# Softmax scaling on GpSimd instead of VectorE, and one f tile in halves, in a dynamic convolution feeding a two-matmul block

## The chip, the cores and the metric

The kernel runs on one core of a Trainium2 chip. The metric is the device time of one execution in microseconds (us). Ten executions of the kernel before had a median of 772.5 us (771.71 to 773.02). Engines are called TensorE (PE in the profile, PEld for its weight loads), VectorE (DVE), ScalarE (ACT), GpSimd (POOL) and SyncE (SP, whose queue issues most DMAs).

## The reference

`x` is (8, 4096, 192) and `weight_gen` is (8, 4096, 8 heads, 7 taps), both float32. Each token has its own softmaxed 7-tap filter per head; the filter runs causally over the sequence, and its output feeds two matmuls with `h - tanh(h)` between them:

```
w = exp(weight_gen - max);  w = w / (sum(w, -1) + 1e-9)
out[b,s,h,:] = sum_k  w[b,s,h,k] * x_pad[b, s+k, h, :]     # 6 zeros in front, 24 channels a head
h = out.reshape(32768, 192) @ w_in          # w_in (192, 2048)
y = (h - tanh(h)) @ w_out                   # w_out (2048, 192), float32 out
```

## The kernel before, in words

Tokens are worked on in 32 *superblocks* of 1024 (`TOK`): partition p holds 8 consecutive tokens (`J`), with a halo of 6 rows in front of them (`HALO`). Four superblocks make one sequence, so every fourth one (`s == 0`) begins with zeros instead of a halo. For each superblock n:

- `load_wg(n)` and `load_x(n)` bring the filter logits and x (with halo) to SBUF through SP's DMA queue. x tiles have two buffers.
- `softmax_exp(n)` takes the exponential on ScalarE (L135). `softmax_norm` (L150) does the rest on VectorE: a sum over taps (L145), a reciprocal (L154), and the *scaling*, exp times reciprocal (L172). The reciprocal is written into the unused end of a PSUM bank: that of the transposes for n >= 4, one of the output banks for 0, 1 and 3. Superblock 2 has a variant, `softmax_norm_gpsimd`, with the reciprocal in SBUF (L166) and the scaling on GpSimd.
- `products(n)` multiplies x, shifted by tap, with the scaled weights: seven products (L195), written in bf16 to `even`, `odd` and `last`. They run on GpSimd, save four of superblock 0 and two of superblock 1, which VectorE does (`on_vector`) with a second copy of the scaled weights in PSUM. From superblock 3 on, a DMA issued by GpSimd (L208) adds `odd` to `even`, the *pair sum*.
- `conv(n)` sums the products and transposes them in one go: matmuls against an identity (L240) accumulate in PSUM, in two parts (channel chunks 0 and 1, then 2), and ScalarE copies them to `convT` (L251).
- `gemm1(n, f)` makes one *f tile*, 128 of the 2048 hidden features for all 1024 tokens: six matmuls (L265) into a PSUM tile `ph`, tanh on ScalarE (L275), subtraction on VectorE into `gt` (L277).
- `gemm2` multiplies 128 tokens of the superblock before with `w_out` (L297), and ScalarE copies the result out (L315); the last superblock has `gemm2_last` (L331).

The order is written out by hand (`manual_schedule`); each engine runs its instructions in program order. The main loop takes superblock n in eight steps p. A step is f tiles 2p and 2p+1, then one block of gemm2 for n-1. At p = 0 the products of n+2 are issued, and from n = 2 on their first one carries an extra dependency, the *pace*: it waits for the subtraction of f tile 1. At p = 5 comes the exponential of n+3, at p = 6 (n >= 2) the transposes of n+1 and then the softmax of n+3.

`ph` and the two PSUM tiles of the transposes (`pc`) come in turn from one pool, `psum_h`, of three buffers. Eighteen tiles a superblock are drawn from it, so in steady state the first part of the transposes takes the buffer of f tile 11, the second that of 12, f tile 14 that of 13, 15 that of the first part, tile 0 of the next superblock that of the second part, and tile 1 that of 14. Each waits until the readers of its predecessor are done.

Weights: `load_w_in` brings `w_in` in two pieces of columns (split at `FA`) to partitions 0 to 63 through GpSimd's queue, and `copy_w_in` copies each piece to partitions 64 to 127, the first from ScalarE's queue, the second from SP's.

Of the kernel before, what the change touches and what calls it, by code (L numbers as in the profile page):

```python
# [16 lines left out]
def kernel(  # L17
# [81 lines left out]
    def load_x(n):  # L99
        b, s = divmod(n, NSB)  # L100
        s0 = s * TOK

        x_t = xpool.tile([P, HALO + J, D], FP32, name="x_t")

        def rows(p0, p1):
            win = x[b, s0 + p0 * J - HALO : s0 + p0 * J - HALO + 1]
            nc.sync.dma_start(
                out=x_t[p0:p1, :, :],
                in_=bass.AP(
                    tensor=win.tensor,  # L110
                    offset=win.offset,
                    ap=[[J * D, p1 - p0], [D, HALO + J], [1, D]],
                ),
            )

        if s == 0:
            nc.sync.dma_start(  # L117
                out=x_t[0:1, 0:HALO, :],
                in_=zero[:].rearrange("o (h d) -> o h d", h=1).to_broadcast([1, HALO, D]),
            )  # L120
            nc.sync.dma_start(
                out=x_t[0:1, HALO : HALO + J, :],
                in_=x[b, 0:J].rearrange("(p j) d -> p j d", p=1),
            )

            rows(1, 16)
            rows(16, P)
        else:
            rows(0, P)
        x_of[n] = x_t  # L130
# [8 lines left out]
        )  # L139
        e_of[n] = e_t  # L140

    def softmax_sum(n):
        e_t = e_of.pop(n)
        zsum = wgpool.tile([P, J * H], FP32, name="zsum")
        nc.vector.reduce_sum(  # L145
            out=zsum[:], in_=e_t[:].rearrange("p j h k -> p (j h) k"), axis=AX.X
        )
        return e_t, zsum

    def softmax_norm(n, bank, in_psum=False):  # L150

        e_t, zsum = softmax_sum(n)
        zr = bank[:, 512 - J * H : 512]
        nc.vector.reciprocal(zr, zsum[:])  # L154
        wsm_v = None
        if in_psum:
            wsm_v = obank[n % 2][:, 0 : J * H * K].rearrange("p (j h k) -> p j h k", j=J, h=H)
            scale(nc.vector, wsm_v, e_t, zr)
        wsm = wgpool.tile([P, J, H, K], FP32, name="wsm")
        last_wsm[0] = scale(nc.vector, wsm[:], e_t, zr)  # L160
        wsm_of[n] = (wsm, wsm_v)

    def softmax_norm_gpsimd(n):
        e_t, zsum = softmax_sum(n)
        zr = wgpool.tile([P, J * H], FP32, name="zr")
        nc.vector.reciprocal(zr[:], zsum[:])  # L166
        wsm = wgpool.tile([P, J, H, K], FP32, name="wsm")
        scale(nc.gpsimd, wsm[:], e_t, zr[:])
        wsm_of[n] = (wsm, None)

    def scale(eng, wsm, e_t, zr):
        return eng.tensor_mul(  # L172
# [2 lines left out]
            zr.rearrange("p (n o) -> p n o", o=1).to_broadcast([P, J * H, K]),  # L175
        )

    def products(n, on_vector=(), sums=None, hooks={}, behind=None):
        x_t = x_of.pop(n)
        wsm, wsm_v = wsm_of.pop(n)  # L180
        in_pairs = n not in PLAIN

        even = ppool.tile([P, NPAIR, NC, J, H, GC], BF16, name="even")
        odd = ppool.tile([P, NPAIR, NC, J, H, GC], BF16, name="odd")
        last = ppool.tile([P, NC, J, H, GC], BF16, name="last")
        dst = {}
        for i in range(NPAIR):
            dst[2 * i] = even[:, i]
            dst[2 * i + 1] = odd[:, i]
        dst[K - 1] = last[:]  # L190
        if -1 in hooks:
            hooks[-1]()
        for k in range(K):
            eng, w = (nc.vector, wsm_v) if k in on_vector else (nc.gpsimd, wsm[:])
            mul = eng.tensor_mul(  # L195
                dst[k].rearrange("p c j h g -> p j h c g"),
                x_t[:, k : k + J, :].rearrange("p j (h c g) -> p j h c g", h=H, c=NC),
                w[:, :, :, k : k + 1]
                .rearrange("p j h (k o) -> p j h k o", o=1)
                .to_broadcast([P, J, H, NC, GC]),  # L200
            )
            if k == 0 and behind is not None:


                order(mul, behind, "pace")
            if k == K - 2 and in_pairs:

                nc.gpsimd.dma_start(  # L208
                    out=even[:].rearrange("p i c j h g -> p (i c j h g)")[:, 0:ACC],
                    in_=odd[:].rearrange("p i c j h g -> p (i c j h g)")[:, 0:ACC],  # L210
                    accum_op=mybir.AluOpType.add,
                    max_dma_last_dim=4096,
                )
            if k in hooks:
                hooks[k]()
        if in_pairs:
            groups = [even[:, i] for i in range(NPAIR)] + [last[:]]
            prods_of[n] = [
                groups + ([odd[:, NPAIR - 1]] if c == NC - 1 else []) for c in range(NC)
            ]  # L220
        else:
            prods_of[n] = [[dst[k] for k in (sums or range(K))]] * NC

    def conv(n, *parts):

        prods = prods_of[n]
        if n not in conv_of:
            conv_of[n] = cpool.tile([P, NC, HT], BF16, name="convT")
        convT = conv_of[n]
        pcs = [psum_h.tile([P, 2, HT], FP32, name="pc", tag="ph") for _ in parts]  # L230

        for gi in range(max(len(g) for g in prods)):
            for chunks, pc in zip(parts, pcs):
                some = [c for c in chunks if gi < len(prods[c])]
                last = gi == max(len(prods[c]) for c in chunks) - 1
                for c in some:
                    for j in range(JH):
                        col = ((c - chunks[0]) * JH + j) * R
                        for r in range(2):
                            nc.tensor.matmul(  # L240
                                pc[:, r, col : col + R],
                                lhsT=prods[c][gi][
                                    r * R : (r + 1) * R, c, 2 * j : 2 * j + 2
                                ].rearrange("p j h g -> p (j h g)"),
                                rhs=ident[r * R : (r + 1) * R, r * R : (r + 1) * R],
                                start=(gi == 0 and c == chunks[0] and j == 0),
                                stop=(last and c == some[-1] and j == JH - 1),
                            )
        for chunks, pc in zip(parts, pcs):
            c0, nch = chunks[0], len(chunks)  # L250
            nc.scalar.activation(  # L251
                out=convT[:, c0 : c0 + nch, :].rearrange("p c (j r t) -> p r (c j) t", r=2, t=R),
                in_=pc[:, :, 0 : nch * JH * R].rearrange("p r (cj t) -> p r cj t", t=R),
                func=ACT.Copy,
            )
        if parts[-1][-1] == NC - 1:
            prods_of.pop(n)
        return pcs[-1][:, 0]

    def gemm1(n, f):  # L260
        convT = conv_of[n]
        ph = psum_h.tile([P, 2, HT], FP32, name="ph", tag="ph")
        for c in range(NC):
# [8 lines left out]
        th = tpool.tile([P, TOK], FP32, name="th")  # L272
        ph_f = ph[:].rearrange("p r t -> p (r t)")
        g1_act[0] = last_act.get(0)
        last_act[0] = nc.scalar.activation(out=th[:], in_=ph_f, func=ACT.Tanh)  # L275
        gt = gpool.tile([P, TOK], BF16, name=f"gt{f}", tag=f"gt{f}")
        last_sub[0] = nc.vector.tensor_sub(gt[:], ph_f, th[:])  # L277
        g_of.setdefault(n, []).append(gt)

    LAST = (NTOT - 1) * J  # L280
# [76 lines left out]
    def load_w_out():  # L357
        nc.gpsimd.dma_start(out=w_out[:], in_=moe_w_out.rearrange("(c p) e -> p c e", c=NFT))

    FA = 8 * P  # L360

    def load_w_in(f0, f1):

        for c in range(NC):
            src = moe_w_in[c * GC : c * GC + 1, f0:f1]
            dma = nc.gpsimd.dma_start(
                out=w_in[0:R, c, f0:f1],
                in_=bass.AP(
                    tensor=src.tensor, offset=src.offset, ap=[[G * F, H], [F, GC], [1, f1 - f0]]
                ),  # L370
            )
            if f0 == 0:

                order(dma, last_wsm[0], "order of the loads")
# [4 lines left out]
    def rest_of_w_in():  # L379
# [2 lines left out]
    load_wg(0)  # L382
    load_x(0)
    softmax_exp(0)
    softmax_norm(0, obank[0], in_psum=True)
    load_wg(1)
    load_x(1)
    load_w_in(0, FA)
    products(
        0,  # L390
        on_vector=(3, 4, 5, 6),
        sums=(3, 0, 4, 5, 1, 6, 2),
        hooks={2: rest_of_w_in},
    )
    softmax_exp(1)
    softmax_norm(1, obank[1], in_psum=True)
    load_wg(2)
    copy_w_in(0, FA, nc.scalar)
    copy_w_in(FA, F, nc.sync)
# [3 lines left out]
    for n in range(NTOT):  # L403
# [1 line left out]
            load_wg(n + 3)  # L405
            load_x(n + 3)
        for p in range(J):
            gemm1(n, 2 * p)
            gemm1(n, 2 * p + 1)
            if n == 0 and p == 1:  # L410
                softmax_exp(2)
# [6 lines left out]
            if n + 1 < NTOT:  # L418
                if p == (6 if n > 0 else 7):
                    conv(n + 1, (0, 1))  # L420
                if p == (6 if n > 1 else 7):
                    bank = conv(n + 1, (2,))
            if n == 0 and p == 2:
                softmax_norm_gpsimd(2)
                products(2)
            if p == (7 if n == 1 else 6) and n + 3 < NTOT:

                softmax_norm(n + 3, bank if n > 0 else obank[0])
    gemm2(LAST)
    for j in range(J):  # L430
        gemm2_last(j)
# [30 lines left out]
```

The softmax here doesn't subtract the row's maximum and nothing guards it: scores larger than these inputs give would overflow.

## Time and profile before

| | |
|---|---|
| median of ten runs | 772.5 us |
| profiled execution | 772.88 us, its span 770.8 us |
| TensorE busy | 741.4 us, 96% of the span |
| VectorE busy | 668.9 us, 87% |
| ScalarE busy | 640.4 us, 83% |
| GpSimd busy | 668.1 us, 87% |
| subtraction (L277) | 512 times 1219 ns |
| tanh (L275) | 512 times 1022 ns |
| scaling on VectorE to SBUF (L172) | 31 times, 620 to 622 ns |
| scaling on GpSimd (L172) | once, 968 ns |
| product on GpSimd (L195) | 218 times, start to start 2.86 us |
| pair sum (L208), issue to landing | 29 times, 8.0 / 8.9 / 10.5 us (least, median, most) |

The span runs from the first to the last instruction of the profiled execution. Busy time counts an instruction from start to end; where consecutive instructions of one engine overlap, the distance between their starts says more. An idle time in brackets is what the engine stood still just before an instruction, with the engine that ended it.

### The profile page before, as it was taken

The page shows a single profiled execution, that of the slowest core. Times are in us where ns is not written, and L with a number is a line of the kernel's source. Part 1 is how long each engine was busy: PE and PEld are TensorE (multiplying, and loading weights), DVE is VectorE, ACT ScalarE, POOL GpSimd, SP SyncE. Part 2 cuts the span into 40 slices and gives each one's busy share as a digit, 9 for nine tenths or more (in the row PEclk, how much of TensorE's full clock was granted, in tenths as well). Part 3 has the DMA queues.
Part 4 walks back from the last instruction along what each step waited for, and adds up shares of the span by engine and source line. Part 5 has one row for each costly group of instructions (what it writes and reads, how often), then busy time and mean ns, then how long its engine had stood idle before and what let it go on. Part 6 is the DMA issues. An engine that isn't in the chain of part 4 may idle for free.

```text
span 770.8 us, 32309 instructions
## 1 busy us (share of the span) xinstructions
PE 741.4 (96%) x14784; PEld 578.8 (75%) x14784; DVE 668.9 (87%) x624; ACT 640.4 (83%) x865; POOL 668.1 (87%) x261
## 2 busy tenths in 40 slices
PE   2789999999999999999999999999999999999997
PEld 2367777777787777778777777777777777778777
DVE  5988889988989898899888998989898988988883
ACT  1777888888888888888888888888888888888882
POOL 5999999999999999999999999999999999999000
PEclk9999999999999999999999999999999999999999
DMA  7913677665557765556765555775555776542312
GB/s 208 192 71 92 177 182 181 157 139 127 152 154 181 182 140 131 136 149 172 181 170 117 131 153 158 181 180 126 135 142 149 178 181 153 133 117 64 82 43 83
DMA packets 25847, 111.37 MB, mean 144 GB/s; under 512 B 4800, under 2 KB 9456, under 8 KB 21624
## 3 DMA queue, kind: packets, MB, share of 16 engines
q1 hardware_dynamic: 14688, 76.95, 30.2%
q0 software_dynamic: 10816, 31.99, 25.7%
q8 instruction: 115, 1.88, 1.0%
q10 hardware_dynamic: 208, 0.39, 0.2%
q14 instruction: 20, 0.16, 0.1%
HBM read 54.49 MB, written 25.17 MB: 103 GB/s over the span
## 4 chain that ended last, share of the span: by engine, by line
PE 93%; DVE 2%; DMA 1%; POOL 1%; issue 1%; ACT 1%; SPq 0%; POOLq 0%; DVEq 0%
PE ph L265 43%; PE obank L297 43%; PE pc L240 6%; DVE gt L277 2%; PE po L331 1%; DMA x_t<-in_x_dram 1%; POOL even L195 1%; ACT convT L251 0%; ACT th L275 0%; POOL odd L195 0%; DVE wsm L172 0%; DVE zsum L145 0%; SPq L117 0%; DVE pc L154 0%; DVE obank L154 0%
## 5 line engine op out<-in xcount | busy, mean ns | idle before, releaser
L277 DVE TENSOR_TENSOR gt<-ph,th 128x1024 bf16<-128x1024 f32 x512 | 602.8, 1219 | 64.0 <-ACT th L275 63.7
L275 ACT ACTIVATE th<-ph 128x1024 f32<-128x1024 f32 x512 | 497.2, 1022 | 65.1 <-PE ph L265 64.7
L265 PE MATMUL ph<-convT,w_in 64*128 64x512 bf16 x3072 | 386.6, 378 | 7.3 <-DVE gt L277 5.0
L297 PEld LDWEIGHTS <-gt 64*128 64x128 bf16 x7936 | 344.4, 94 | 52.3 <-ACT th L275 0.8
L297 PE MATMUL obank<-w_out,gt 64*128 64x192 bf16 x7936 | 374.0, 243 | 1.4 <-issue 0.6
L195 POOL TENSOR_TENSOR even<-x_t,wsm 128x1536 bf16<-128x1536 f32 x94 | 276.8, 2945 | 30.6 <-DVE gt L277 28.6
L195 POOL TENSOR_TENSOR odd<-x_t,wsm 128x1536 bf16<-128x1536 f32 x93 | 273.8, 2944 | 0.0
L265 PEld LDWEIGHTS <-w_in 64*128 64x128 bf16 x3072 | 176.5, 94 | 117.4 <-issue 21.3
L195 POOL TENSOR_TENSOR last<-x_t,wsm 128x1536 bf16<-128x1536 f32 x31 | 103.4, 3334 | 0.0
L315 ACT ACTIVATE out_sb<-obank 128x192 f32<-128x192 f32 x248 | 81.9, 330 | 13.9 <-PE obank L297 8.6
L251 ACT ACTIVATE convT<-pc 128x1024 bf16<-128x1024 f32 x64 | 48.6, 808 | 30.7 <-PE pc L240 30.7
L240 PE MATMUL pc<-ident,even 64*128 64x64 bf16 x2304 | 47.4, 191 | 2.9 <-DVE gt L277 1.5
L240 PEld LDWEIGHTS <-even 64*128 64x128 bf16 x2304 | 42.5, 96 | 3.8 <-issue 1.9
L208 POOL DMA_DIRECT2D even<-odd x29 | 34.9, 1205 | 9.0 <-POOL odd L195 9.0
L154 DVE RECIPROCAL pc<-zsum 128x64 f32<-128x64 f32 x28 | 15.7, 561 | 14.7 <-ACT convT L251 14.6
L240 PE MATMUL pc<-ident,odd 64*128 64x64 bf16 x448 | 15.2, 198 | 13.0 <-DVE odd L195 13.0
L135 ACT ACTIVATE e_t<-wg_t 128x448 f32<-128x448 f32 x32 | 18.5, 577 | 8.3 <-DMA wg_t<-in_weight_gen_dram 8.3
L240 PE MATMUL pc<-ident,last 64*128 64x64 bf16 x768 | 23.1, 191 | 0.8 <-issue 0.7
L145 DVE TENSOR_REDUCE zsum<-e_t 128x64 f32<-128x448 f32 x32 | 19.5, 610 | 2.8 <-ACT e_t L135 2.8
L240 PEld LDWEIGHTS <-odd 64*128 64x128 bf16 x448 | 11.2, 100 | 13.2 <-DVE odd L195 13.1
L172 DVE TENSOR_TENSOR wsm<-e_t,pc 128x448 f32<-128x448 f32 x28 | 17.4, 622 | 2.9
L240 PEld LDWEIGHTS <-last 64*128 64x128 bf16 x768 | 17.0, 96 | 1.1 <-issue 0.8
(22 smaller groups left out, 51.4 us busy)
## 6 DMA issues: line engine op xcount, KB each, us to landing
x_t<-in_x_dram SPq DMA_DIRECT2D x24, 1344.0 KB
even<-odd POOLq DMA_DIRECT2D x29, 1024.0 KB, 8.9
out_dram<-out_sb SPq DMA_DIRECT2D x31, 768.0 KB
x_t<-in_x_dram SPq DMA_DIRECT2D x8, 1176.0 KB
wg_t<-in_weight_gen_dram SPq DMA_DIRECT2D x32, 224.0 KB
x_t<-in_x_dram SPq DMA_DIRECT2D x8, 157.5 KB
w_in<-in_moe_w_in_dram POOLq DMA_DIRECT2D x6, 128.0 KB, 7.0
w_out<-in_moe_w_out_dram POOLq DMA_DIRECT2D x1, 768.0 KB, 9.7
```

The source lines that it names most:

```text
L135: nc.scalar.activation(out=e_t[:].rearrange("p j h k -> p (j h k)"), in_=wg_t[:].rearrange("p j h k -> p (j h k)"), func=ACT.Exp,)
L145: nc.vector.reduce_sum(out=zsum[:], in_=e_t[:].rearrange("p j h k -> p (j h) k"), axis=AX.X)
L172: return eng.tensor_mul(wsm.rearrange("p j h k -> p (j h) k"), e_t[:].rearrange("p j h k -> p (j h) k"), zr.rearrange("p (n o) -> p n o", ...
L195: mul = eng.tensor_mul(dst[k].rearrange("p c j h g -> p j h c g"), x_t[:, k : k + J, :].rearrange("p j (h c g) -> p j h c g", h=H, c=NC), ...
L208: nc.gpsimd.dma_start(out=even[:].rearrange("p i c j h g -> p (i c j h g)")[:, 0:ACC], in_=odd[:].rearrange("p i c j h g -> p (i c j h g)" ...
L240: nc.tensor.matmul(pc[:, r, col : col + R], lhsT=prods[c][gi][r * R : (r + 1) * R, c, 2 * j : 2 * j + 2].rearrange("p j h g -> p (j h g)") ...
L251: nc.scalar.activation(out=convT[:, c0 : c0 + nch, :].rearrange("p c (j r t) -> p r (c j) t", r=2, t=R), in_=pc[:, :, 0 : nch * JH * R].re ...
L265: nc.tensor.matmul(ph[:, r, :], lhsT=w_in[r * R : (r + 1) * R, c, f * P : (f + 1) * P], rhs=convT[r * R : (r + 1) * R, c, :], start=(c == ...
L275: last_act[0] = nc.scalar.activation(out=th[:], in_=ph_f, func=ACT.Tanh)
L277: last_sub[0] = nc.vector.tensor_sub(gt[:], ph_f, th[:])
L297: mm = nc.tensor.matmul(po[:, 0:D], lhsT=g_of[n][f][r * R : (r + 1) * R, col : col + P], rhs=w_out[r * R : (r + 1) * R, f, :], start=(r == ...
L315: last_act[0] = nc.scalar.activation(out=out_sb[:, j, :], in_=po[:, 0:D], func=ACT.Copy)
```

## The change

- *Scaling.* The normalisation of superblocks 0 and 1 stays as it was, on VectorE. For all others `softmax_norm(n)` now ends with the reciprocal, in an SBUF tile; the scaling is issued on GpSimd as the first instruction of `products(n)`, and the pace is put on it instead of on the first product. The softmax of n+3 stands at p = 6 in every superblock (n = 1 had it at p = 7).
- *Halves.* f tile 12 of superblocks 1 to 30, the first of the two f tiles of the step that ends with the transposes, goes through tanh and subtraction in two halves of 512 tokens.
- *Beginning.* x of superblock 0 is loaded first without halo for all partitions, then the halo in two pieces, then the zeros of partition 0. Its products are issued in the order 6, 0, 3, 1, 4, 5, 2 (VectorE: 6, 3, 4, 5; GpSimd: 0, 1, 2), and the transposes sum them in the order 6, 3, 0, 4, 5, 1, 2. The first piece of `w_in` has seven f tiles instead of eight, the second nine.

```diff
+        def rows(p0, p1, r0=0, r1=HALO + J):
+            win = x[b, s0 + p0 * J - HALO + r0 : s0 + p0 * J - HALO + r0 + 1]
...
+        if n == 0:
+            rows(0, P, HALO, HALO + J)
+            rows(16, P, 0, HALO)
+            rows(1, 16, 0, HALO)
+            no_halo()
+        elif s == 0:
+            no_halo()
+            rows(0, 1, HALO, HALO + J)
             rows(1, 16)
             rows(16, P)
...
-    def softmax_norm(n, bank, in_psum=False):
+    def softmax_norm(n, bank=None):
         e_t = e_of.pop(n)
         zsum = wgpool.tile([P, J * H], FP32, name="zsum")
         nc.vector.reduce_sum(...)
+        wsm = wgpool.tile([P, J, H, K], FP32, name="wsm")
+        if bank is None:
+            zr = wgpool.tile([P, J * H], FP32, name="zr")
+            nc.vector.reciprocal(zr[:], zsum[:])
+            wsm_of[n] = (wsm, None, e_t, zr)
+            return
...
-    def products(n, on_vector=(), sums=None, hooks={}, behind=None):
+    def products(n, on_vector=(), order_of=None, sums=None, hooks={}, behind=None):
         x_t = x_of.pop(n)
-        wsm, wsm_v = wsm_of.pop(n)
+        wsm, wsm_v, e_t, zr = wsm_of.pop(n)
+        if e_t is not None:
+            first = scale(nc.gpsimd, wsm[:], e_t, zr[:])
+            if behind is not None:
+                order(first, behind, "pace")
...
-        for k in range(K):
+        for k in order_of or range(K):
...
-            if k == 0 and behind is not None:
-                order(mul, behind, "pace")
...
-    def gemm1(n, f):
+    def gemm1(n, f, parts=1):
...
-        last_act[0] = nc.scalar.activation(out=th[:], in_=ph_f, func=ACT.Tanh)
-        last_sub[0] = nc.vector.tensor_sub(gt[:], ph_f, th[:])
+        for q in range(parts):
+            t0, t1 = q * TOK // parts, (q + 1) * TOK // parts
+            last_act[0] = nc.scalar.activation(
+                out=th[:, t0:t1], in_=ph_f[:, t0:t1], func=ACT.Tanh
+            )
+            last_sub[0] = nc.vector.tensor_sub(gt[:, t0:t1], ph_f[:, t0:t1], th[:, t0:t1])
...
-    FA = 8 * P
+    FA = 7 * P
...
-        on_vector=(3, 4, 5, 6),
-        sums=(3, 0, 4, 5, 1, 6, 2),
+        on_vector=(6, 3, 4, 5),
+        order_of=(6, 0, 3, 1, 4, 5, 2),
+        sums=(6, 3, 0, 4, 5, 1, 2),
...
-            gemm1(n, 2 * p)
+            gemm1(n, 2 * p, 2 if p == 6 and 0 < n < NTOT - 1 else 1)
...
-            if p == (7 if n == 1 else 6) and n + 3 < NTOT:
-                softmax_norm(n + 3, bank if n > 0 else obank[0])
+            if p == 6 and n + 3 < NTOT:
+                softmax_norm(n + 3)
```

## The prediction

> **What bounds the kernel now.** I read the page first (busy time, then the chain that ended last), and then the timeline of one superblock from the middle. From the page:
>
> ```profile
> PE 741.4 (96%) x14784; PEld 578.8 (75%) x14784; DVE 668.9 (87%) x624; ACT 640.4 (83%) x865; POOL 668.1 (87%) x261
> PE 93%; DVE 2%; DMA 1%; POOL 1%; issue 1%; ACT 1%; SPq 0%; POOLq 0%; DVEq 0%
> ```
>
> TensorE carries 93% of the chain. A change of VectorE or GpSimd work can therefore pay only where TensorE waits for them. The timeline around one set of transposes (L240) shows where that is; columns: start us, duration us, engine, line, instruction, and in brackets the idle time before it.
>
> ```profile
> 361.18 1.48 PE L265 MATMUL ph<-convT,w_in 64*128 64x512 bf16 x12
> ...
> 363.11 2.36 DVE L277 TENSOR_TENSOR gt<-ph,th 128x1024 bf16<-128x1024 f32 x2 [0.26 <-ACT th L275]
> ...
> 363.80 0.88 PE L240 MATMUL pc<-ident,even 64*128 64x64 bf16 x48
> ...
> 365.51 1.47 PE L265 MATMUL ph<-convT,w_in 64*128 64x512 bf16 x12
> 366.37 1.94 ACT L275 ACTIVATE th<-ph 128x1024 f32<-128x1024 f32 x2
> 366.49 0.56 DVE L154 RECIPROCAL pc<-zsum 128x64 f32<-128x64 f32 x1 [0.51 <-ACT convT L251]
> ...
> 367.16 0.62 DVE L172 TENSOR_TENSOR wsm<-e_t,pc 128x448 f32<-128x448 f32 x1
> 367.69 4.71 DVE L277 TENSOR_TENSOR gt<-ph,th 128x1024 bf16<-128x1024 f32 x4
> ...
> 368.13 1.67 PE L265 MATMUL ph<-convT,w_in 64*128 64x512 bf16 x12
> ...
> 370.93 1.48 PE L265 MATMUL ph<-convT,w_in 64*128 64x512 bf16 x12
> ```
>
> A regular step (two f tiles and one output block) is 2.61 us, as from 358.57 to 361.18. Eight steps (20.92) and the transposes (1.52 in the chain) make 22.44. But the same row returns every 22.82 us (365.51, 388.33). The missing 0.38 has two halves.
> (a) Transposes start at 363.80, so the next f tile (14) could start at 365.32; it starts at 365.51. It takes the PSUM buffer of tile 13, whose subtraction ends at 363.11 + 2.36 = 365.47: a wait of 0.19.
> (b) 368.13 to 370.93 is 2.80, 0.19 too long. Tile 1 of the new superblock takes the buffer of tile 14, whose subtraction starts at 367.69, late, behind the reciprocal and the scaling. As a check: superblock 29 has transposes but no softmax behind them, and its period (707.95 to 730.58) is 22.63, exactly (b) less.
>
> GpSimd, third:
>
> ```profile
> 36.32 0.97 POOL L172 TENSOR_TENSOR wsm<-e_t,zr 128x448 f32<-128x448 f32 x1
> 37.37 2.90 POOL L195 TENSOR_TENSOR even<-x_t,wsm 128x1536 bf16<-128x1536 f32 x1
> ...
> 78.59 3.35 POOL L195 TENSOR_TENSOR even<-x_t,wsm 128x1536 bf16<-128x1536 f32 x1
> ...
> 100.16 3.36 POOL L195 TENSOR_TENSOR even<-x_t,wsm 128x1536 bf16<-128x1536 f32 x1
> ...
> 349.66 2.90 POOL L195 TENSOR_TENSOR even<-x_t,wsm 128x1536 bf16<-128x1536 f32 x1 [1.19 <-DVE gt L277]
> ```
>
> Unpaced, GpSimd's round is 100.16 - 78.59 = 21.57; later it waits about 1.19 per round for the pace. The one scaling that it does today takes it 37.37 - 36.32 = 1.05 from start to start.
>
> [...] the scaling at 36.32 ran beside back-to-back subtractions, so 1.05 holds for the loop. [...]
>
> **The change part by part.**
>
> *Scaling off VectorE (29 scalings, those of 3 to 31, issued in superblocks 0 to 28; that of 2 was on GpSimd already).* It removes 0.62 us and the reciprocal's 0.51 wait for the copy of the transposes, since the reciprocal now goes to SBUF (0.55, row L166). Sum and reciprocal run 365.38 to about 366.55; VectorE is then free, and tile 14's subtraction starts when its tanh ends (366.37 + 1.02, about 367.43) instead of at 367.69. That alone would lift (b), but with (a) lifted too tile 14 starts earlier, while ScalarE still copies the transposes until 366.46 and can't start its tanh before 366.37. I leave 0.08 of the 0.19 standing: gain 0.11 in 27 superblocks, 3.0 us.
>
> *Tile 12 in halves (n = 1 to 30).* Tanh of 512 columns costs about 0.59 (row convT 128x512), so two take about 0.06 more ScalarE time than one of 1.02[...]. The first half can start at about 362.8 (when tile 11's is done) instead of 363.11, so tile 13's subtraction is no longer queued behind tile 12's but starts when its own tanh ends, 0.15 earlier. Gain 0.15 of (a)'s 0.19 in 29 superblocks (2 to 30; superblock 1 splits its transposes otherwise, taken as nothing): 4.35 us.
>
> *Scaling on GpSimd, pace ahead of it.* 21.57 + 1.05 = 22.62 per round, against TensorE's new 22.56. The 1.19 of pace wait covers it, and more: products never catch up with the pace after superblock 4, so that wait is gone and GpSimd runs without a break. Does the conv then wait for products? Products(4) would start near 78.9 (78.59 + 1.05 - 0.7 from the beginning), products(31) at 78.9 + 27 x 22.62 = 689.6; the pair sum is issued 1.05 + 17.5 later and lands 8.9 (median row) to 10.5 after that: 717.1 to 718.7. The last transposes, at 728.86 now, come at about 720.5. So the cover is 2 to 3.5 us at the end. Behind products on SP stand the x load, an output store and a weight_gen load; each moves later by GpSimd's lag behind the pace, at most 6 us by these starts, and each has over 10 us until its reader (the x load about 22.6 less its landing). Without cover the kernel would end at GpSimd's speed: 717.9 + 42 (what follows the last transposes now) = 760 span.
>
> *Beginning.* x of superblock 0 comes without halo first, then the halo; the two tiny transfers no longer stand ahead. VectorE can start k = 6 near 7 to 8 us; GpSimd starts k = 0, which needs the halo, near 9.8 instead of 10.52 (bounds: 9.3, if all of the 1.2 us that SP spends on the tiny ones, 1.19 to 2.43, is won; 10.7, if the shorter rows cost as much as that), and its three products still end last on the way to the transposes. Tile 0 of the first matmul at 20.92 also waited for the copy of w_in (1.05, landing 20.9), which is 7/8 as big now. I take 0.6 for both. The second part of w_in, 9/8 as big, is now needed for tile 7 (at 30.0 now): its copy was issued at 26.02, the first one took 3.7 us, so it lands at about 29.5: cost 0.3 (0 to 1.0). VectorE sets the pace in superblock 0 (12 waits of L265 for L277, 5.0 us, nearly all before 41 us); it loses one scaling: 0.6. Superblock 2's first step loses 0.2 of (b).
>
> *Sum.* 3.0 + 4.35 + 0.6 + 0.6 + 0.2 - 0.3 = 8.4. Span 770.8 - 8.4 = 762.4; its execution 772.88 - 8.4 = 764.5. Against the median of ten, 772.5, that is 764.1.
>
> **Rivals.**
> 1. *Both halves of the wait vanish and GpSimd becomes the bound.* Period 22.44 would give 28 x 0.38 + 1.1 = 11.7 off, but products for 31 land at 717.9: end at 760 span, 762 measured; with the early landing 760.5. For it: my residues 0.08 and 0.04 are small differences of large numbers. Against: ScalarE's copies stay where they are. 15%.
> 2. *The halves do nothing.* If the second half waits as long as the whole did, only the scaling pays: (b) goes fully, 27 x 0.19 + 1.1 = 6.2: 766.3, or 769 if the beginning also loses 1.6 us, to w_in's second copy above all, where I have it gain 1.1. For it: the idle that it uses is 0.26 only[...]. 17%.
> 3. *Slower: the scaling is dearer in the loop.* GpSimd then sets the period. Its end is 728.9 + 29 x s - 0.7 for a start-to-start price s; it equals 770.8 at s = 1.47. At s = 1.7 it is 777.5 span, 779 measured. For it: only one sample of s exists. Against: it was taken beside busy VectorE. 9%.
> 4. *Nothing moves,* since a new wait of the same size replaces each: 772 +- 1.5. The 22.63 of superblock 29 speaks against it. 4%.
>
> **How the numbers follow.** Main case 55% (762.5 to 766, its range from w_in's 0 to 1.0, the beginning's bounds and residues of 0 to 0.1), rivals 15, 17, 9 and 4. Rivals 1 and 2 and the main case are faster: 87%; rival 4 is same, rival 3 slower. 0.2% is 1.5 us, about what this kernel's runs can tell. The range goes from rival 1's lower end, 760.3, to 769, rival 2's far end.
>
> **What would show it.** GpSimd's pace waits go from 28.6 us to nearly nothing; a GpSimd scaling row x30 of about 0.97; GpSimd rounds of 22.6; TensorE period 22.5 to 22.6; reciprocals without a wait for convT; tile 14's tile pair starting under 1.58 us after the transposes. Wrong: transposes waiting for GpSimd or for the pair sum in the last third; a scaling above 1.2; a tile-7 wait over 1 us near 30 us.

## The result, and the profile after

The changed kernel takes 788.47 us (median; 788.12 to 788.58) against 772.73 of the kernel before: a ratio of 1.0203, with a 95% interval of 1.0194 to 1.0212. It is 15.7 us slower; 764.1 was predicted, 760.3 to 769.0. The profiled span grew from 770.8 to 785.8.

First the page of the changed kernel: busy time with the number of instructions, then the chain that ended last.

```profile
PE 740.1 (94%) x14784; PEld 581.9 (74%) x14784; DVE 657.5 (84%) x625; ACT 641.0 (82%) x895; POOL 696.2 (89%) x290
PE 69%; DVE 18%; ACT 8%; issue 3%; POOL 1%; DMA 0%
```

TensorE does the same work in the same busy time, but carries 69% of the chain instead of 93%. VectorE, 2% before, has 18%, ScalarE 8%. So work that leads from VectorE over ScalarE back to TensorE has got onto the path, although both engines stand idle for longer than before (VectorE 128 us of the span for 102, ScalarE 145 for 130). GpSimd's busy time rose by 28.1 us for 29 scalings, as it should; it is 1% of the chain.

The view of all waits, columns: waiting engine, its tile and line, engine and line waited for, us in all, times, longest us.

```profile
ACT th L276 <- DVE gt L279: 24.9, 30, 0.8
PE ph L262 <- DVE gt L279: 23.2, 40, 1.4
POOL wsm L168 <- DVE gt L279: 14.9, 21, 0.7
```

The first row did not exist before: 30 times a tanh waits for a subtraction, 0.83 us each, although a tanh reads nothing that a subtraction writes. 30 is the number of f tiles in halves. In the second row TensorE waits for subtractions, 23.2 us where it was 5.0. The third is GpSimd at the pace: it still waits in 21 of the 28 superblocks whose products carry a pace, so it was not late there.

The timeline of one superblock from the middle, tile 12 to the head of the next; columns as in the prediction.

```profile
365.42 2.95 DVE L279 TENSOR_TENSOR gt<-ph,th 128x1024 bf16<-128x1024 f32 x3 [0.26 <-ACT th L276]
366.11 1.47 PE L262 MATMUL ph<-convT,w_in 64*128 64x512 bf16 x12
...
366.97 0.60 ACT L276 ACTIVATE th<-ph 128x512 f32<-128x512 f32 x1
...
368.40 1.51 ACT L276 ACTIVATE th<-ph 128x512 f32<-128x512 f32 x2 [0.83 <-DVE gt L279]
368.73 0.88 PE L238 MATMUL pc<-ident,even 64*128 64x64 bf16 x48
369.03 0.69 DVE L279 TENSOR_TENSOR gt<-ph,th 128x512 bf16<-128x512 f32 x1 [0.66 <-ACT th L276]
...
369.95 1.23 DVE L279 TENSOR_TENSOR gt<-ph,th 128x1024 bf16<-128x1024 f32 x1 [0.22 <-ACT th L276]
...
371.23 1.47 PE L262 MATMUL ph<-convT,w_in 64*128 64x512 bf16 x12 [0.69 <-DVE gt L279]
...
373.84 1.48 PE L262 MATMUL ph<-convT,w_in 64*128 64x512 bf16 x12
...
394.65 1.47 PE L262 MATMUL ph<-convT,w_in 64*128 64x512 bf16 x12 [0.69 <-DVE gt L279]
```

Read it along tile 12. Its first tanh ends at 367.57. VectorE is busy with tiles 10 and 11 and comes to the first half last in its row of three, which ends at 365.42 + 2.95 = 368.37. Only then, at 368.40, does the second tanh start: ScalarE stood still for 0.83 us with tile 12's second half ready in PSUM. Everything behind is late by this: the second subtraction (369.03), tile 13's tanh and subtraction (369.95 to 371.18), and tile 14's matmuls, which need tile 13's buffer: 371.23, or 2.50 us after the transposes' start at 368.73. That distance was 1.71 before, and 1.52 is the work itself. The period is 394.65 - 371.23 = 23.42, where it was 22.82.

The pair behind tile 14 starts 2.61 later (373.84), and so does the next: wait (b), tile 1 of the new superblock, is gone, as predicted. So 23.42 = 22.44 + 0.98 of wait (a), where it was 22.44 + 0.19 + 0.19.

The sum over the span: superblock 1 starts at 42.34 instead of 45.41 (3.07 won at the beginning). From there to the f tile behind the last transposes (tile 14 of superblock 30) it takes 703.58 instead of 685.17: 18.4 lost, 29 x 0.60 = 17.4 of it in the periods. What follows is 0.35 shorter. 18.4 - 3.1 - 0.35 = 15.0.

### The profile page after: what moved, and what is told of

Read it like the earlier page. It is cut to its first block, busy times and chain, and to the rows that moved or that the text cites. A ratio compares the mean times of both kernels' runs of the same rounds, so it can differ in the third digit from the quotient of the medians.

```text
span 785.8 us, 32390 instructions
## 1 busy us (share of the span) xinstructions
PE 740.1 (94%) x14784; PEld 581.9 (74%) x14784; DVE 657.5 (84%) x625; ACT 641.0 (82%) x895; POOL 696.2 (89%) x290
## 4 chain that ended last, share of the span: by engine, by line
PE 69%; DVE 18%; ACT 8%; issue 3%; POOL 1%; DMA 0%
PE ph L262 35%; PE obank L299 32%; DVE gt L279 17%; ACT th L276 8%; PE po L333 1%; POOL even L197 1%; PE pc L238 1%; DMA wg_t<-in_weight_gen_dram 0%; DVE zsum L150 0%; ACT convT L249 0%; POOL w_in L368 0%; DVE zr L156 0%; POOL odd L197 0%; DVE obank L168 0%; DVE wsm L168 0%
## 5 line engine op out<-in xcount | busy, mean ns | idle before, releaser
L279 DVE TENSOR_TENSOR gt<-ph,th 128x1024 bf16<-128x1024 f32 (+1 forms) x542 | 607.4, 1161 | 108.9 <-ACT th L276 108.7
L276 ACT ACTIVATE th<-ph 128x1024 f32<-128x1024 f32 (+1 forms) x542 | 502.2, 974 | 105.9 <-PE ph L262 80.6
L262 PE MATMUL ph<-convT,w_in 64*128 64x512 bf16 x3072 | 381.9, 377 | 24.6 <-DVE gt L279 23.2
L197 POOL TENSOR_TENSOR even<-x_t,wsm 128x1536 bf16<-128x1536 f32 x94 | 272.9, 2903 | 2.4
L197 POOL TENSOR_TENSOR odd<-x_t,wsm 128x1536 bf16<-128x1536 f32 x93 | 270.0, 2903 | 0.0
L238 PEld LDWEIGHTS <-even 64*128 64x128 bf16 x2304 | 44.4, 96 | 5.8 <-POOL even L197 3.1
L168 POOL TENSOR_TENSOR wsm<-e_t,zr 128x448 f32<-128x448 f32 x30 | 31.8, 1059 | 14.9 <-DVE gt L279 14.9
L238 PE MATMUL pc<-ident,last 64*128 64x64 bf16 x768 | 23.2, 191 | 9.4 <-DVE last L197 8.3
L156 DVE RECIPROCAL zr<-zsum 128x64 f32<-128x64 f32 x30 | 16.6, 553 | 3.3 <-DVE zsum L150 0.5
```

What stands on the lines that cost most here:

```text
L168: return eng.tensor_mul(wsm.rearrange("p j h k -> p (j h) k"), e_t[:].rearrange("p j h k -> p (j h) k"), zr.rearrange("p (n o) -> p n o", ...
L197: eng.tensor_mul(dst[k].rearrange("p c j h g -> p j h c g"), x_t[:, k : k + J, :].rearrange("p j (h c g) -> p j h c g", h=H, c=NC), w[:, : ...
L238: nc.tensor.matmul(pc[:, r, col : col + R], lhsT=prods[c][gi][r * R : (r + 1) * R, c, 2 * j : 2 * j + 2].rearrange("p j h g -> p (j h g)") ...
L262: nc.tensor.matmul(ph[:, r, :], lhsT=w_in[r * R : (r + 1) * R, c, f * P : (f + 1) * P], rhs=convT[r * R : (r + 1) * R, c, :], start=(c == ...
L276: last_act[0] = nc.scalar.activation(out=th[:, t0:t1], in_=ph_f[:, t0:t1], func=ACT.Tanh)
L279: last_sub[0] = nc.vector.tensor_sub(gt[:, t0:t1], ph_f[:, t0:t1], th[:, t0:t1])
```

## The experiments

The theory after the result: the second half waits for the first because both belong to one PSUM tile, `ph`, and the program orders any two engines' accesses to it. Its rivals: they are tied by `th`, the SBUF tile that both halves share; or the loss comes with the scaling on GpSimd, and the wait is only where it shows. A second question came up on the way: where 6 us stayed that the shorter periods should have won.

### Tile 12 whole

```diff
-            gemm1(n, 2 * p, 2 if p == 6 and 0 < n < NTOT - 1 else 1)
+            gemm1(n, 2 * p)
```

> The change with f tile 12 whole again; scaling on GpSimd and the new beginning stay. Theory (the halves' second tanh waits for the first subtraction, and that alone made the loss): the wait of ScalarE for VectorE before L276, 24.9 us in 30 waits, is gone; half (b) of the old stall is gone and half (a) stays, so the period falls from 23.42 to about 22.63 us, and with the beginning's 3 us the time is 763 to 767 us. Rival (GpSimd's scaling costs the time): the period stays above 23 us and the time stays above 780 us.

768.64 us, 0.9947 (0.993 to 0.9963) of the kernel before. Taking the halves back wins 19.8 us, though the time is 1.6 above the expected range. Its timeline:

```profile
362.94 0.87 PE L238 MATMUL pc<-ident,even 64*128 64x64 bf16 x48
...
364.64 1.47 PE L262 MATMUL ph<-convT,w_in 64*128 64x512 bf16 x12
...
366.56 2.36 DVE L279 TENSOR_TENSOR gt<-ph,th 128x1024 bf16<-128x1024 f32 x2 [0.79 <-ACT th L276]
367.26 1.48 PE L262 MATMUL ph<-convT,w_in 64*128 64x512 bf16 x12
...
372.22 1.42 POOL L168 TENSOR_TENSOR wsm<-e_t,zr 128x448 f32<-128x448 f32 x1
```

Tile 14 starts 1.70 after the transposes, the old (a); its subtraction waits for its own tanh and for nothing else, and the pairs follow at 2.62: (b) is gone. The period is 22.63, the figure that superblock 29 of the kernel before had shown. So the scaling is not what made the changed kernel slower.

### Each part alone, on the kernel before

The halves alone; the new beginning alone; the scaling of superblocks 3 to 31 on GpSimd alone (with the softmax of superblock 4 at p = 6).

> The kernel before with only the halves of f tile 12 added. Theory: the second tanh is held by the first subtraction here too, so the wait (a) of 0.19 us grows to about 0.98 as in the changed kernel, and (b) stays about 0.19 because the scaling is still on VectorE: period about 23.6 us, 29 x 0.8 = 23 us more, 788 to 797 us. Rival (the halves only hurt together with GpSimd's scaling): 771 to 776 us.

> The kernel before with only the new beginning (load order, order of the products, w_in split). The changed kernel reached superblock 1 at 42.34 us instead of 45.41; 0.6 of that is the scaling. Theory: superblock 1 starts 2.4 us earlier here, period 22.82 unchanged; all of it kept gives 770.1 us. If TensorE loses part of it again in superblocks 1 to 4 without a wait that the profile names, 771 to 772 us.

> The kernel before with only the scaling of superblocks 3 to 31 on GpSimd. Theory: (b) of the stall is gone, period 22.63 us: 27 x 0.19 + 0.6 = 5.7 us less, 766.8 us; with unnamed TensorE stalls as in the run with f tile 12 whole (5.1 us in all against 1.3 before), up to 770 us. Rival (the scaling's 1.05 us on GpSimd delays the transposes): a period over 22.8 us with transposes waiting for GpSimd or the pair sum, 773 us or more.

| part | us | ratio to before |
|---|---|---|
| halves | 789.06 | 1.0216 (1.0201 to 1.0232) |
| beginning | 771.48 | 0.9984 (0.9977 to 0.9991) |
| scaling | 770.81 | 0.9978 (0.9969 to 0.9987) |

The halves alone cost 16.5 us, more than the whole change. A row of their timeline, the end of wait (a) after transposes at 369.70:

```profile
372.20 1.47 PE L265 MATMUL ph<-convT,w_in 64*128 64x512 bf16 x12 [0.69 <-DVE gt L281]
```

2.50 after the transposes again, and the period is 23.41, although the scaling is still on VectorE; 23.6 was expected, with (b) on top. That is why the parts don't add up: with tile 14 this late, (b) is hidden, and moving the scaling away wins nothing in the loop. The scaling alone was to win 5.7 by the periods (28 x 0.19 and a little in superblock 0) and won 1.7; the second question begins here.

### What ties the halves

Each half with a `th` tile of its own:

```diff
-        th = tpool.tile([P, TOK], FP32, name="th")
...
         for q in range(parts):
             t0, t1 = q * TOK // parts, (q + 1) * TOK // parts
+            th = tpool.tile([P, TOK], FP32, name="th")
...
```

> The change, with a tanh tile of its own for each half. Theory A (the second tanh is held because it writes the same SBUF tile th that the first subtraction reads): the wait before the half tanh vanishes and the time falls to 761 to 766 us. Theory B (it is held because both read the same PSUM tile ph): nothing changes, 788 us, period 23.42 us, 0.83 us of wait before each second half.

788.38 us, 1.0202 (1.0187 to 1.0217), and the wait of tanh for subtraction is still there, 30 times and 24.8 us. It is not `th`; of what the two instructions touch, `ph` alone is left in common.

Both tanhs issued ahead of both subtractions:

> The change, with both half tanhs issued ahead of both half subtractions. By theory B the order is then reversed: the first subtraction is held until the second tanh has read ph, so ScalarE isn't held but nothing starts earlier than with a whole tile, and the halves cost only their fixed parts, about 0.1 us a superblock: period about 22.7 us, 766 to 770 us. By theory A the first subtraction would wait for both tanhs as well, with the same time. If neither holds and the halves are dear in themselves: above 780 us.

772.08 us, 0.9992 (0.9983 to 1.0001). Now the order is turned round:

```profile
362.49 2.01 ACT L276 ACTIVATE th<-ph 128x512 f32<-128x512 f32 x3
...
363.61 2.42 DVE L281 TENSOR_TENSOR gt<-ph,th 128x512 bf16<-128x512 f32 x3 [0.32 <-ACT th L276]
364.25 0.88 PE L238 MATMUL pc<-ident,even 64*128 64x64 bf16 x48
...
366.08 1.47 PE L262 MATMUL ph<-convT,w_in 64*128 64x512 bf16 x12
```

The tanhs run through, but the first subtraction starts only when the second tanh is done (363.61), not after the first (363.1). Tile 14 comes 1.83 after the transposes, later than with a whole tile. Here the wait does not tell the two tiles apart, since the first subtraction shares both `ph` and `th` with the second tanh. What it shows is that the order of issue decides which of the two engines waits. The period is 22.75.

The same, with that one order declared unnecessary:

```diff
+            tanh_q = nc.scalar.activation(...)
+            if q > 0:
+                tc.declare_no_dep(tanh_q.ins, last_sub[0].ins, reason=...)
...
```

> The change, with the order between the second half's tanh and the first half's subtraction left undrawn[...]. Theory: the first-half subtraction starts 0.3 to 0.4 us earlier than a whole one, the 0.83 us wait is gone, and the prediction's arithmetic applies: period 22.5 to 22.6 us, 761 to 765 us. Rival (halves are dear for another reason, such as ScalarE's added fixed time in front of the copies of the transposes): a period of 22.7 us or more, 767 us or more.

768.45 us, 0.9944 (0.9929 to 0.9958).

```profile
359.26 4.82 DVE L282 TENSOR_TENSOR gt<-ph,th 128x1024 bf16<-128x1024 f32 x5 [0.26 <-ACT th L276]
...
360.81 2.00 ACT L276 ACTIVATE th<-ph 128x512 f32<-128x512 f32 x3
...
362.57 0.87 PE L238 MATMUL pc<-ident,even 64*128 64x64 bf16 x48
...
364.13 1.48 PE L262 MATMUL ph<-convT,w_in 64*128 64x512 bf16 x12
```

The wait of tanh for subtraction is gone. ScalarE goes through both halves and tile 13 in one row of three, VectorE through tiles 10, 11, both halves and 13 in one row of five. Tile 14 starts 1.56 after the transposes, so 0.04 of (a) is left, and the period is 22.54. These are the prediction's residues (0.04 and 0.08, 22.56). Tile 12 in two parts lets tile 14 start 0.14 us sooner here (1.56 after the transposes for 1.70 with the whole tile), and 0.80 later where the parts were tied (2.50).

This also says what the order was: one that the programming layer had drawn for this pair; without it the same 30 pairs ran as well. That it draws it from the shared tile `ph` follows by elimination, `th` having been ruled out. Here ScalarE reads one half of `ph` while VectorE reads the other: the second tanh and the first subtraction overlap by 0.37 us or more in each of the 30 tiles. Two engines in one half at once were not tried.

### The 6 us that were missing

Without the tie (the order between the halves), the period is 0.28 shorter than before: 28 of them are 7.8 us, with the 2.5 of the beginning 10.3. Only 4.3 came out. The expected ranges say the same: whole tile 12, both tanhs first, the scaling alone and no tie all came out slower than their ranges, by 0.8 to 3.5 us. The difference lies mostly in the first seven superblocks, where TensorE stands still with no wait that the profile can name ("issue"; *unnamed idle* below, counted from 0.15 us up, as the views list it). The rows of TensorE with such an idle, in the kernel before:

```profile
68.72 0.90 PE L297 MATMUL obank<-w_out,gt 64*128 64x192 bf16 x17 [0.58 <-issue]
...
113.59 0.26 PE L240 MATMUL pc<-ident,last 64*128 64x64 bf16 x6 [0.68 <-issue]
```

and the four longest of five in the one with the whole tile 12:

```profile
66.73 0.90 PE L299 MATMUL obank<-w_out,gt 64*128 64x192 bf16 x17 [1.60 <-issue]
...
91.61 0.91 PE L299 MATMUL obank<-w_out,gt 64*128 64x192 bf16 x17 [0.79 <-issue]
...
112.85 0.26 PE L238 MATMUL pc<-ident,last 64*128 64x64 bf16 x6 [1.17 <-issue]
...
159.47 0.27 PE L238 MATMUL pc<-ident,even 64*128 64x64 bf16 x7 [1.52 <-issue]
```

That is 1.3 us in all before and 5.4 with the whole tile 12; without the tie it is 5.8, so 4.5 of the 6 us. These idles stop TensorE in the midst of a row of like matmuls, where there is no data to wait for, in the transposes or within some 3 us behind a part of them. The page has one more thing on the transfer engines, a queue of instructions (queue, packets, MB, share of the transfer engines):

```profile
q8 instruction: 115, 1.88, 1.0%
```

115 blocks of 16,384 bytes, and TensorE runs 2 x 14,784 = 29,568 matmuls and weight loads. If the blocks are TensorE's, that is 115 x 16,384 / 29,568 = 63.7, so about 64 bytes for each and 256 to a block (an estimate from these counts). With 64 or more instructions put in front, as below, there are 116 blocks. Each of these idles ends 2.1 to 2.8 us after the start of such a block. The one that ends at 159.47 has its block in this stretch of 0.2 us, beside the transfers of SP's queue:

```profile
q1 hardware_dynamic: 28, 0.07, 83.0%
q8 instruction: 1, 0.02, 29.2%
```

The blocks themselves take 0.9 to 2.0 us each, with or without an idle behind them, so it is their start that comes late. A step uses 88 instructions in 2.61 us, the transposes 208 in 1.52, four times as many per us, and in or close behind them these idles stand. What makes a block late? Either its edge falls near the transposes, or something else holds it.

*Edges moved.* 32, 64 or 96 more matmuls in front shift the edges by a quarter, half or three quarters of a block; their result is overwritten.

> The change with f tile 12 whole, and 64 spare matmuls (128 instructions of TensorE) in front, in time in which TensorE stands idle; their result is overwritten. Theory F (TensorE's unnamed idle times in superblocks 1 to 6, 1.60 + 0.79 + 1.17 + 1.52 us, are a late supply of instructions: blocks of 16 KB, 256 instructions, come on a queue of their own, and one ends about 1.3 us before each of these stalls): the half block of shift moves them to other places, and the time changes by 0.5 us or more either way, 765 to 770 us. Rival D (they are waits for data, the pair sum or x): they stay at 66.7, 91.6, 112.9 and 159.5 us with the same sizes, and the time stays within 0.4 us of 768.6.

> The halves without the order between them (768.45 us), with 32 spare matmuls (64 instructions, a quarter of a 16 KB block) in front. By theory F the unnamed idle times of TensorE, 5.3 us in all, depend on where the blocks' edges fall against the transposes: they move, 766 to 770 us. Were they waits for data, 768.5 us with idle times at 67.0, 91.6 and 113.3 us.

> As the run with 32, but 96 spare matmuls (three quarters of a block): by theory F the idle times of TensorE stand at other places again and the time is 766 to 770 us; a place with few edges inside transposes would bring it near the 763 that the prediction's arithmetic gives.

769.75 with the whole tile (0.9967, 0.9954 to 0.998); 768.53 and 768.82 without the tie (both 0.9949). The idles moved, with 64 more to 43.8, 66.6, 91.9 and 137.2 us among others; the two near 66.7 and 91.6 now stand within the transposes, where they stood behind them. But there were as many us of them: 5.5 for 5.4 with the whole tile, 6.4 and 5.9 for 5.8 without the tie. Where they stand depends on the edges; how much they cost hardly does.

*The scaling twice.* The scaling on GpSimd done two times over, tile 12 whole.

> The change with f tile 12 whole and the scaling done twice on GpSimd, the second time over the first. Theory (one scaling is covered by the pace's wait, and the prediction's sum for GpSimd's end is right): GpSimd's round is 21.57 + 2.10 = 23.67 us, it becomes the bound, and the last transposes wait for the pair sum of 31, started near 719 and landing near 747: 42 us later the span ends at about 789, 787 to 793 us measured. Rival (GpSimd has far more room than the sum gives it): 768 to 771 us.

796.57 us, 1.0313 (1.0298 to 1.0328), against the 787 to 793 expected. GpSimd's rows:

```profile
340.85 2.48 POOL L168 TENSOR_TENSOR wsm<-e_t,zr 128x448 f32<-128x448 f32 x2
364.55 2.48 POOL L168 TENSOR_TENSOR wsm<-e_t,zr 128x448 f32<-128x448 f32 x2
```

Its round is 23.70, which is 22.64 + 1.06 as worked out, and TensorE's mean period is 23.7 too. But in the loop TensorE does not wait for a product or a pair sum: its idle has no name again, 26.3 us over the kernel. Behind three of these idles (2.63, 1.89 and 2.47 us) the granted clock was 0.5 for 3.4 us each, which costs some 5 us more (an estimate: half of 3 x 3.4). What GpSimd does shift is the x load, which starts when its products are done with an x buffer. The share of the transfer engines (second figure from the right) in the 4 us ahead of a set of transposes, from the views of the kernel before, the whole tile 12 and the double scaling, one row each:

```profile
154.40:158.40 4.00, 4.00 (x80) 3.38 (x77) 3.48 (x4) 4.00 (x6) 4.00 (x2) 1.00 0.26 98
```

```profile
153.20:157.20 4.00, 4.00 (x81) 3.39 (x78) 3.48 (x4) 4.00 (x6) 4.00 (x2) 1.00 0.90 298
```

```profile
346.80:350.80 4.00, 4.00 (x80) 3.33 (x76) 3.48 (x4) 4.00 (x6) 4.00 (x2) 1.00 0.97 257
```

Before, SP's transfers (x load, output, weight_gen) run from 11.6 to 3 us ahead of the transposes; with the whole tile 12 from 9.1 to 0.4 ahead, in the first superblocks to 3 after; with the double scaling from about 6 ahead to 3 after. The closer they run to the transposes and over them, the more unnamed idle TensorE has in these three: 1.3, 5.4 and 26.3 us. Not every such set of transposes has one: with the whole tile 12, a share of 0.92 ahead of those at 134.5 us left none.

*The x load placed there on purpose.* The kernel before, x of superblock n+3 held until f tile 7's subtraction of n:

```diff
-            load_x(n + 3)
+            if n == 0:
+                load_x(n + 3)
...
+            if p == 3 and 0 < n < NTOT - 3:
+                load_x(n + 3, late=last_sub[0])
```

> The kernel before with the x load of superblock n+3 held until the subtraction of f tile 7 of superblock n, so that it lies from about 6 us before the transposes to 4 after their start, where it lay from 11.6 to 3 before them. It still ends over 4 us before the products that read it. Theory 'x load over the transposes': unnamed idle of TensorE at the transposes in most superblocks, 8 to 20 us in all where there was 1.3, and 778 to 790 us. Theory 'block edges alone': no change beyond 1 us, 771.5 to 773.5.

777.66 us, 1.0064 (1.0044 to 1.0084): 5.3 slower, just short of the 778 to 790 expected, and far from no change. The load now ran up to the transposes, in some superblocks up to 1 us over them, and not 4 us over them as expected; unnamed idles stood in 11 superblocks and came to 7.9 us. Two of the rows:

```profile
184.04 0.29 PE L242 MATMUL pc<-ident,odd 64*128 64x64 bf16 x7 [0.99 <-issue]
438.04 0.48 PE L242 MATMUL pc<-ident,even 64*128 64x64 bf16 x21 [1.25 <-issue]
```

*The x load taken away, first try.* A third buffer for x (`bufs=3`), so that the load need not wait for the products of two superblocks before.

> The kernel with the order between the halves taken away, and a third buffer for x, so that the x load no longer waits for the products of two superblocks before and starts at the head of a superblock. Theory 'x load over the transposes': TensorE's instruction blocks start late while an x load is under way; without the third buffer the load lies from about 8 us before the transposes to 0.5 after their start. Moved away, the unnamed idle of TensorE falls from 6.4 us to under 2, the superblock's period stays at 22.54, and the time is 763.5 to 765.5 us. Theory 'block edges alone' (an edge of a block in or near the transposes is late wherever the x load is): the idle stays at about 5 to 6, and the time at 768 to 769. A third way: the pair sum, now beside the x load, lands several us later, and TensorE waits for it by name.

> The kernel before with a third buffer for x alone. There the x load already ends about 3 us ahead of the transposes from superblock 6 on, and only in the first few does it overlap them. Theory 'x load over the transposes': the unnamed idle goes from 1.3 us to nearly 0, 771 to 772.5 us. Theory 'block edges alone': no change, 772.5. It is mainly the control for the third buffer in the other kernels: alone it is worth at most 1.5 us.

> The scaling done twice on GpSimd, tile 12 whole, and a third buffer for x. With two buffers the x load lay from about 6 us before to 3 us after the start of the transposes, and TensorE had some 20 us of unnamed idle. Theory 'x load over the transposes': that idle goes to under 3 us, and TensorE waits for the pair sum by name instead once its lead is used up; GpSimd still needs 23.7 us a superblock, so the time falls only to what GpSimd allows, 787 to 795 us. Theory 'block edges alone': the unnamed idle stays near 20 us and the time at 796.5.

769.38 (0.9955), 775.87 (1.004, 1.0026 to 1.0054) and 793.39 us (1.0269). The first two miss their ranges; the third lies in its range, but not for the reason given, since most of its unnamed idle stayed. With three buffers the load comes one superblock earlier but at the same place in it, since it still starts where GpSimd's products end. And at the start two x loads ran beside the load of w_out, which without the tie landed 18.9 us after its issue instead of 9.5; TensorE then stood 2.7 us for it, and ran 6.8 us at half the granted clock after that. The unnamed idle did fall: 5.8 to 3.1 us without the tie, 1.3 to nothing in the kernel before, 26.3 to 16.2 with the double scaling.

*Second try.* Three buffers, and the x load of superblock n+4 held until f tile 13's subtraction of n, just after the transposes; those of 3 and 4 held to tile 9 of superblock 0 and tile 1 of superblock 1.

```diff
-            load_x(n + 3)
...
+            if n < 2 and p == (4, 0)[n]:
+                load_x(n + 3, held=last_sub[0])
+            if n > 0 and p == 6 and n + 4 < NTOT:
+                load_x(n + 4, held=last_sub[0])
```

> The kernel with the order between the halves taken away, a third buffer for x, and the x load of superblock n+4 held until the subtraction of f tile 13 of superblock n, so that it runs from about 2 to 10 us after the start of the transposes, with the pair sum behind it and nothing over the next transposes; x of superblocks 3 and 4 are held too (to tiles 9 and 1), so that the load of w_out is not delayed as it was with the third buffer alone, where TensorE stood 2.7 us for w_out and then ran 6.8 us at half its clock. Theory 'x load over the transposes': the unnamed idle of TensorE falls from 5.9 us to under 1, the period is 22.54, and the time 763 to 765 us. Theory 'block edges alone': the idle stays at 4 to 6 us, 767.5 to 769 us. A third way: loads and pair sum now overlap for longer, the pair sum lands later, and TensorE waits for it by name.

> The kernel before with the same third buffer and held x loads, as the control. Its x loads already ended 3 us ahead of the transposes except in the first superblocks, so the theory 'x load over the transposes' allows 1.3 us at most: 771 to 772.5 us; 'block edges alone' expects 772.5. If the held loads cost something of their own, it shows here.

762.05 us, 0.9862 (0.9849 to 0.9876), 1 below the expected range, and 771.5 for the control, 0.9982 (0.9975 to 0.9989). The rows of the 4 us ahead of the same set of transposes without the tie, first as it was (transposes at 157.6), then with the loads held (at 153.3):

```profile
153.60:157.60 4.00, 4.00 (x81) 3.39 (x78) 3.74 (x5) 4.00 (x7) 4.00 (x2) 1.00 0.95 320
149.30:153.30 4.00, 4.00 (x81) 3.41 (x79) 3.74 (x5) 4.00 (x7) 4.00 (x3) 1.00 0.09 15
```

A share of 0.09 instead of 0.95, no unnamed idle in the whole kernel instead of 5.8 us, and a period of 22.54 from superblock 4 on. The control gains 1.3, the idle that the kernel before had, and has none left either. So the place of the x load decides; that the instruction blocks queue behind its packets is the likely way, and is argued, not shown. From superblock 21 on some periods are 22.6 to 22.8, and one 23.3, with a wait for the pair sum by name:

```profile
PE pc L240 <- DMA even<-odd: 0.7, 1, 0.7
```

GpSimd's round of 22.64 against 22.54 has then used up its lead.

## Why the prediction was wrong

- **Tile 12 in halves** is the step that failed: "The first half can start at about 362.8 ... so tile 13's subtraction is no longer queued behind tile 12's but starts when its own tanh ends, 0.15 earlier". It took the halves as independent, that is, it put the wait between them at nothing. They share `ph`, and in the order that the program draws the second tanh waits for the first subtraction, 0.83 us, and the term that was to win 4.35 us lost 16.5 (halves alone). The premise that they are independent was never put as an unknown. What the halves cost by themselves was the author's estimate; without the tie it is 0.06 for ScalarE (a row of two halves and a whole tile 2.00, one of two whole tiles 1.94) and 0.11 for VectorE (three whole tiles and two halves 4.82, four whole tiles 4.71), and the step gives what it said: tile 14 at 1.56, a period of 22.54.
- **Scaling off VectorE** (3.0) was right in mechanism: (b) is gone in every kernel that has it. In the changed kernel it is worth nothing in the loop, since the halves' delay covers (b).
- **Scaling on GpSimd**: a round of 22.62 was predicted, 22.64 measured. The scaling itself is recorded with 0.97 behind a pace wait and with 1.42 where it directly follows a product, so that "a scaling above 1.2" was no good sign of being wrong: the round is the same. The pace waits did not go, 14.9 us of them are left, only because the superblock became longer than the round; with tile 12 whole there are none. The cover of 2 to 3.5 us at the end fits the last superblocks of the fastest kernel, where it is used up.
- **Beginning**: up to the start of superblock 1 the sum had 0.6 + 0.6 - 0.3 = 0.9, and 3.07 was measured (1.0 with the new beginning alone, 1.4 with the scaling alone); the term was too small. The two do not add up to 3.07, and why is open. VectorE starts k = 6 at 6.48 and GpSimd k = 0 at 8.79, below the lower bound of 9.3; the first matmul starts 1.7 earlier. The wait feared at tile 7 did not come, since the second w_in copy too is issued 2.1 earlier (23.91 for 26.02).
- **What lies on SP behind the products** was costed at nothing, "each moves later by GpSimd's lag ... and each has over 10 us until its reader". True of the readers, but the load's own passage ahead of and over the transposes costs TensorE 4 to 5 us without a wait that has a name. It would have made 768 of 764 had the halves been independent. That 762.05 lies below 764.1 once both are mended is mostly the beginning, 2.7 up to superblock 1 there where the sum had 0.9.
- **Rivals.** Rival 2 said that the halves do nothing, not that they cost. For the halves I had no bound below nothing. Rival 3, the slower one, named the scaling, and that did not happen (22.64 per round). Rivals 1 and 4 did not come about. The cases that end faster had 87% in all because none of them let the halves cost anything.

## What to carry to other kernels

Cutting an instruction in two to let the next engine start earlier can leave both parts on one tile: before counting the gain, ask which order the program draws between the second half on the first engine and the first half on the second, and look in the first trace for a wait of the producer on its consumer (here 30 times 0.83 us). A moved instruction also moves the transfers that wait for its engine. In the transposes here, where TensorE works off 208 instructions in 1.52 us, keeping the x load away took 5.8 us of unnamed idle to nothing: try it where instructions are as short, and read an idle time without a named releaser against the share of the transfer engines ahead of it (0.95 and 0.09 here).

## What the runs showed of the hardware

The profile shows instructions on the same transfer engines as the data, in 115 blocks of 16,384 bytes in the kernel before and in the changed one, each 0.9 to 2.0 us long. All 112 unnamed idle times of TensorE in the traces of these kernels, 0.16 to 4.45 us, ended 2.1 to 2.8 us after a block's start; they grew from 1.3 to 7.9 us in all when nothing but the x load was moved up to the transposes, and fell from 5.8 to nothing when, with a third buffer for x, it was held until behind their start. That TensorE runs out of instructions there is the reading that fits; the queue itself is not seen.

Behind idle times of 1.9 to 4.5 us the granted clock fell to 0.5 for 3.4 us, in eight places of the two kernels with the double scaling. Behind waits of 2.4 and 2.7 us for w_out, in the two others with a third buffer and no held loads, it did so for 6.8 us. Behind an idle of 3.12 us, in the run with 32 spare matmuls, it stayed full. So the length alone does not decide.

ScalarE and VectorE reading different halves of one PSUM tile at once, for 0.37 us or more in each of 30 tiles, did not slow each other: half a subtraction took 0.68 us and half a tanh 0.59, against 0.69 and 0.60 in the changed kernel, in which they took turns.
